# Decode attention with a mixer MLP on one core: K of the filling unit ahead of a batch's last V, queries with wq as weights, a ring of 16 cells

## The chip, the cores and the metric

One core of a Trainium2 chip runs the whole program in one launch. The metric is the device time in microseconds of one execution. Before the change the median of three runs is 2520.77 us (2520.22 to 2522.88).

## What is computed

Two rounds of the same layer pair on two batch rows of 512 numbers: attention over a cached K and V of 32768 places (8 groups of heads, 4 query heads each, 128 numbers a head), then an MLP whose hidden size is 1792 and which works on each number of the row by itself (one token, S = 1). The cache and the weights are the same in both rounds.

```python
x = x + A(layernorm(x))      # attention: q = x @ wq; softmax(q k / sqrt(128)) v; @ wo
x = x + B(layernorm(x))      # u[d, f] = layernorm(x)[d] * w1[f] + b1[f]; gelu(u) @ w2 + b2
x = x + A(layernorm(x))
x = x + B(layernorm(x))
```

K and V are 2 x 2 x 8 x 32768 x 128 floats, 537 MB, and each is read again in the second round.

## The kernel before, in words

A *unit* (layer, batch, group of heads) is the attention of one batch row over one group's cache: 64 cells of K and 64 of V, a cell being 128 partitions x 512 floats (256 KB). There are 32 units. SBUF holds `CELLS` = 105 such cells in one tile, `mem` (line 219). Weights (wq and wo of a group, 8 cells) share it.

The work of the array is a list of 1024 *steps* (class `Order`, line 41), each of four cells: `k_step` (line 315) multiplies four K cells by the unit's query (which stands as weights in `qz`) into scores in PSUM, `v_step` (line 366) multiplies four V cells by the exponentials `S` into `acc`. In general the K steps of a unit stand ahead of the V steps of the unit before, so that the maxima (`max_1`, `max_2`), the transposition of the scores (`turn_scores`, VectorE) and the exponentials (`exponentials`, ScalarE, a half of 32 cells at a time) have other steps beside them. Where K of a unit is followed by its own V, everything hangs on one step: there `p1 == p2` (line 665) and the planner adds 5 us.

Second-round K and V of a batch need the batch's whole first round: the last V of that batch, its output (`take_out`, `out_1`, `out_2`), the layer norm (`mix_1`, `take_rows`, `mix_2`), 14 hidden tiles of 128 x 512 (`hidden_tiles`: gelu on ScalarE, projection on TensorE), `mix_4`, `to_columns`, and the new query (`make_q`). At each of the two places where a batch changes its layer (`changes`), three units take part: x, whose V is the batch's last; the *filling unit* of the other batch, whose steps stand beside the chain; and y, which is the same group and batch as x in the second round and uses again what of x's K and V has stayed in SBUF (`KEPT_K` = 8 cells of K and `KEPT_V` = 64 of V). Before, the order there is: K of x, V of the unit before, first half of the filling unit's K, V of x, second half of the filling unit's K, its V, K of y, V of y.

Small pieces of work are *hooks* put behind chosen steps (function `at`, line 627; from line 659 on for each unit), with an estimate of their time in us. TensorE executes steps and hooks in this order; the other engines get their instructions in the same order.

Loads are planned ahead of time by `plan_loads` (line 112): in the order in which the cells are asked for, each load takes 32, 24, 16, 8 or 4 cells (or the sizes that `cut` has set) at the place where, by the planner's model (`CELL_US`, `LAND_US`, `LEAD_US`, `STEP_US`), DMA would wait least, and is issued by the SP engine right behind the last step that used those cells (lines 722 and 744). Cells that neither hold weights nor stay for y are the ring: near the changes 105 - 72 - 16 = 17 cells, which are loaded four at a time.

`make_q` (line 280) is given one unit or two (both batches of a group): in steps 0 and 1 two matmuls each with the row as weights (128 x n) and wq as the moving operand (512 columns), result n x 512; a copy; in step 2 four transpositions by matmul, and copies into `qz`.

Of the kernel before, what the change touches and what calls it, by code (L numbers as in the profile page):

```python
# [8 lines left out]
F32 = mybir.dt.float32  # L9
AF = mybir.ActivationFunctionType  # L10
# [3 lines left out]
P = 128  # L14
G = 512
# [1 line left out]
STEP = 4  # L17
NG = 4
QT = 4
CELLS = 105  # L20
WCELLS = 8
KEPT_K = 8
KEPT_V = 64
SIZES = (32, 24, 16, 8, 4)
FINAL = (16, 8, 4, 2, 1, 1)
# [7 lines left out]

LOAD_US = 0.12
CELL_US = 0.6024
LAND_US = 1.0
LEAD_US = 2.5
STEP_US = 1.44


class Order:


    def __init__(self, heads):
        far, f, s = list(range(heads - 2)), heads - 2, heads - 1
        self.steps = []
        self.pairs = []
        before = [(0, b, h) for h in far for b in (0, 1)] + [(0, 0, f)]
        x0, fill0, y0 = (0, 0, s), (0, 1, f), (1, 0, s)
        x1, fill1, y1, n = (0, 1, s), (1, 0, f), (1, 1, s), (1, 1, f)  # L50
        after = [(1, b, h) for h in far[:1:-1] for b in (0, 1)] + [(1, b, h) for b in (0, 1) for h in far[1::-1]]
        for i, u in enumerate(before):
            self.k(u)
            if i:
                self.v(before[i - 1])
        self.k(x0), self.v(before[-1]), self.k(fill0, 0), self.v(x0), self.k(fill0, 1), self.v(fill0)
        self.k(y0), self.v(y0), self.k(x1), self.k(fill1, 0), self.v(x1), self.k(fill1, 1), self.v(fill1)
        self.k(y1), self.v(y1), self.k(n)
        prev = n
        for u in after:  # L60
            self.k(u), self.v(prev)
            prev = u
        self.v(prev)
        self.last = prev
        self.changes = ((x0, fill0, y0), (x1, fill1, y1))
        self.units = before + [x0, fill0, y0, x1, fill1, y1, n] + after
        self.first, self.end = {}, {}
        for p, (kind, u, g) in enumerate(self.steps):
# [26 lines left out]

# [99 lines left out]
def gqa_mixer_kernel(ctx: ExitStack, tc: tile.TileContext, x, kt, v, wqo, cols, out):  # L195
# [22 lines left out]
    nc.sync.dma_start(xcols, x)  # L218
    mem = const.tile([P, CELLS * G], F32, name="mem")

    def cells(a, n):
# [52 lines left out]
    def row_tile():  # L274
        return work.tile([P, D], F32, name="row", bufs=1)

    wq_sb, wo_sb = {}, {}
    q_at, q_ps, q_row, turn = {}, {}, {}, [0]

    def make_q(us, step):  # L280

        layer, b, h = us[0]
        n = len(us)
        wq = wq_sb[layer, h] if (layer, h) in wq_sb else wq_sb[0, h]
        if step == 0:
            q_ps[us] = pmisc.tile([P, G], F32, name="misc")
        if step < 2:
            for d in range(step * DT // 2, (step + 1) * DT // 2):
                nc.tensor.matmul(  # L289
                    q_ps[us][:n, :], xn[layer][:, d, b : b + n], wq[:, d, :], start=(d == 0), stop=(d == DT - 1)  # L290
                )
        if step == 1:
            q_row[us] = row_tile()
            nc.vector.tensor_copy(q_row[us][:n, :], q_ps[us][:n, :])  # L294
        if step == 2:
            pt = pmisc.tile([P, G], F32, name="misc")
            for r in range(R):
                nc.tensor.matmul(  # L298
                    pt[:, r * n : (r + 1) * n],
                    q_row[us][:n, r * DH : (r + 1) * DH],  # L300
                    ident[:n, :n],
                    start=True,
                    stop=True,
                )
            for j, u in enumerate(us):
                q_at[u] = 28 + 32 * (turn[0] % SLOTS)
                turn[0] += 1
                nc.vector.tensor_copy(
                    qz[:, q_at[u] : q_at[u] + R], pt[:, : n * R].rearrange("p (r b) -> p b r", b=n)[:, j, :]
                )  # L310

    sc_ps, mx, lsum, oT = {}, {}, {}, {}
    at_cell = {}
# [171 lines left out]
    def gelu_table():  # L485
        t = work.tile([P, 1], F32, name="warm", bufs=1)
        nc.scalar.activation(t, one, AF.Gelu_apprx_tanh)

    hid = {}

# [140 lines left out]
    def queries(us, p0, p1, p2):  # L631
        at(p0, make_q, us, 0, us=1.3)
        at(p1, make_q, us, 1, us=1.3)
        at(p2, make_q, us, 2, us=1.0)

    changed = {y: (x, fill) for x, fill, y in order.changes}
    opening = order.units[0]
# [2 lines left out]
    for u in order.units:  # L640
        layer, b, h = u
        users.setdefault(h if h >= HKV - 2 else (layer, h), []).append(u)
        k0 = first["K", u]
        if u in made and u != opening:
            continue
        mate = (layer, 1, h)
        us = (u, mate) if b == 0 and mate not in made and (layer == 0 or h < HKV - 2) else (u,)
        made.update(us)
        if u == opening:
            opening_q = us  # L650
        elif u not in changed:
# [7 lines left out]
    for u in order.units:  # L659
# [17 lines left out]
        at(v_mid + 2, denominators, u, us=0.2)  # L677
        at(v_end, take_out, u)
        if u == order.last:
            at(v_mid + 4, gelu_table)  # L680
            at(v_mid + 3, mix_1, key, us=0.8)
            at(v_end, out_1, u)
            at(v_end, last_mixer, u)
            continue
        at(v_end + 1, out_1, u, us=1.0)
        at(v_end + 2, out_2, u, us=2.4)
        if u == order.last_of[key]:
            e = v_end
            at(e + 1, mix_1, key, us=0.8)
            at(e + 3, take_rows, key)  # L690
            at(e + 4, mix_2, key, us=0.7)
            g0 = e + 9
            for k in range(FT // 2 + 1):
                at(g0 + k, hidden_tiles, key, k, us=1.0)
            g0 += FT // 2
            at(g0 + 1, take_rows, key)
            at(g0 + 2, mix_4, key, us=0.7)
            if layer == 0:
                at(g0 + 3, to_columns, key, us=0.5)
                (y,) = [y for y, (x, _) in changed.items() if x == u]  # L700
                queries((y,), g0 + 4, g0 + 5, g0 + 6)
                assert g0 + 6 < first["K", y]
# [25 lines left out]
    begin = {}  # L728
    for label, n, a, p in loads:
        begin.setdefault(p, []).append((label, n, a))  # L730
    for label, n, a in begin.get(-1, ())[:1]:
        load(label, n, a)
    nc.sync.dma_start(cols_sb, cols)
    for label, n, a in begin.get(-1, ())[1:]:
        load(label, n, a)
    constants()
    first_input()
    for step in range(3):
# [52 lines left out]
```

## Time and profile before

| | us |
|---|---|
| median of 3 runs | 2520.77 |
| profiled execution | 2520.16 |
| its span, first to last instruction | 2518.4 |
| TensorE busy with matmuls | 1442.3 (57%) |
| TensorE loading weights | 400.0 (16%) |
| VectorE busy | 181.3 (7%) |
| ScalarE busy | 183.7 (7%) |
| from HBM | 1065.38 MB, 423 GB/s over the span |

PE is TensorE's matmuls, PEld its weight loads, DVE VectorE, ACT ScalarE, POOL GpSimd, SP the engine that issues loads. One float32 matmul stands in the trace as two records, so that a step of four cells is 8 records. A row of the timeline has the start, the busy time, engine, line, operation, result and operands, number of records, and in brackets how long the engine was idle before and what ended that. A row of the table of stretches has the stretch and its length, the busy times of PE, PEld, DVE, ACT and POOL (records in brackets), the granted clock of TensorE as a share of full speed, the share of DMA, and GB/s.

### The profile page before, as it was taken

To read this page: it belongs to the slowest core of one execution; us is meant where nothing else is said; L and a number is where in the kernel's file an instruction comes from. 1 tells how busy PE (TensorE), PEld (TensorE's weight loads), DVE (VectorE), ACT (ScalarE), POOL (GpSimd) and SP (SyncE) were. 2 spreads that over 40 slices of the span, in tenths; PEclk is the share of its full clock that TensorE was granted. 3 is DMA by queue.
4 is the path that set the end of the run, shared out by engine and by line. 5 is a ranking of instruction groups with operands and counts; after the bars stand their busy time and mean duration, and the time that the engine had idled before them with its cause. 6 is when DMAs were issued, how large, how long until landed. Compare 5 with 4: busy or idle time off the path is not lost.

```text
span 2518.4 us, 20745 instructions
## 1 busy us (share of the span) xinstructions
PE 1442.3 (57%) x9484; PEld 400.0 (16%) x9484; DVE 181.3 (7%) x473; ACT 183.7 (7%) x572; POOL 4.9 (0%) x16
## 2 busy tenths in 40 slices
PE   4455555655556545557686785455564545565566
PEld 1111111111111111112121221111111111111122
DVE  1000000000000000000100010000000000000011
ACT  0000000000000000002011101000000000000021
POOL 0000000000000000000000000000000000000000
PEclk7777777777767777778887787777777777777777
DMA  9999999999999999999999999999999999999996
GB/s 416 432 436 434 434 431 432 431 431 431 431 433 433 433 435 433 418 435 396 403 427 398 397 425 430 438 434 431 431 433 433 434 430 438 434 426 433 426 430 258
DMA packets 33792, 1066.71 MB, mean 424 GB/s; under 512 B 4005, under 2 KB 4009, under 8 KB 4394
## 3 DMA queue, kind: packets, MB, share of 16 engines
q1 hardware_dynamic: 33700, 1065.40, 98.8%
q8 instruction: 74, 1.21, 0.2%
q14 instruction: 12, 0.10, 0.0%
q10 hardware_dynamic: 6, 0.00, 0.0%
HBM read 1065.38 MB, written 0.00 MB: 423 GB/s over the span
## 4 chain that ended last, share of the span: by engine, by line
DMA 67%; PE 31%; ACT 1%; DVE 1%; issue 0%; SPq 0%; POOLq 0%; ACTq 0%; DVEq 0%
DMA mem<-in_kt_dram 36%; DMA mem<-in_v_dram 30%; PE acc L375 12%; PE scores L322 12%; PE misc L420 2%; PE rows L437 2%; PE misc L289 1%; ACT S L357 0%; PE rows L493 0%; PE misc L346 0%; PE misc L340 0%; PE bcast L457 0%; PE acc L592 0%; PE misc L539 0%; PE bcast L519 0%
## 5 line engine op out<-in xcount | busy, mean ns | idle before, releaser
L375 PE MATMUL acc<-mem,S 128*16 128x512 f32 x4092 | 626.7, 711 | 523.0 <-DMA mem<-in_v_dram 513.3
L322 PE MATMUL scores<-mem,qz 128*32 128x512 f32 x4096 | 613.4, 734 | 524.9 <-DMA mem<-in_kt_dram 524.8
L357 ACT ACTIVATE S<-S,neg 128x128 f32<-128x128 f32 x256 | 129.6, 509 | 2247.1 <-DVE S L352 1180.9
L322 PEld LDWEIGHTS scores<-mem,qz 128*32 128x32 f32 x4096 | 136.8, 128 | 926.0 <-DMA mem<-in_kt_dram 469.2
L375 PEld LDWEIGHTS acc<-mem,S 128*16 128x16 f32 x4092 | 129.9, 106 | 848.3 <-issue 793.1
L332 DVE TENSOR_REDUCE mx<-scores 128x1 f32<-128x512 f32 x64 | 44.3, 692 | 827.9 <-PE scores L322 827.9
L289 PE MATMUL misc<-mem,xn 128*2 128x512 f32 (+1 forms) x144 | 86.9, 737 | 4.3 <-DMA mem<-in_wqo_dram 4.3
L420 PEld LDWEIGHTS misc<-selg,row 128*128 128x128 f32 x256 | 50.8, 295 | 46.8 <-issue 41.6
L352 DVE STREAM_TRANSPOSE S<-scores 128x512 f32<-128x512 f32 x64 | 45.5, 711 | 140.7 <-PE acc L375 140.7
L420 PE MATMUL misc<-selg,row 128*128 128x4 f32 x256 | 53.6, 333 | 0.6 <-DVE row L405 0.6
L437 PE MATMUL rows<-mem,oT 128*1 128x512 f32 x248 | 52.1, 931 | 0.0
L357 ACT ACTIVATION_READ_ACCUMULATOR S<-S,neg 128x1 f32 x256 | 47.7, 187 | 0.0
L493 PE MATMUL rows<-hid,cols_sb 128*1 128x512 f32 x84 | 33.8, 616 | 1.0 <-ACT hid L508 1.0
L342 DVE TENSOR_REDUCE m<-misc 1x4 f32<-1x128 f32 x32 | 8.9, 278 | 342.4 <-PE misc L340 342.4
L415 DVE COPY row<-acc 128x512 f32<-128x512 f32 x31 | 21.5, 692 | 149.7 <-PE acc L375 149.7
L508 ACT ACTIVATE hid<-bcast,bias,scale 128x512 f32<-128x512 f32 x42 | 30.4, 774 | 17.0 <-PE rows L493 8.6
L289 PEld LDWEIGHTS misc<-mem,xn 128*2 128x2 f32 (+1 forms) x144 | 14.5, 101 | 74.2 <-issue 72.9
L428 DVE TENSOR_TENSOR oT<-misc,rl 128x4 f32<-128x4 f32 x32 | 5.2, 162 | 283.6 <-PE misc L420 283.6
L294 DVE COPY row<-misc 2x512 f32<-2x512 f32 (+1 forms) x18 | 12.2, 679 | 183.5 <-PE misc L289 123.0
L340 PE MATMUL misc<-ident,mxa 128*1 128x128 f32 x64 | 17.8, 375 | 5.1 <-DVE mxa L338 5.1
L401 DVE RECIPROCAL rl<-misc 128x4 f32<-128x4 f32 x32 | 5.9, 183 | 197.4 <-PE misc L399 197.4
L298 PEld LDWEIGHTS misc<-ident,row 2*128 2x128 f32 (+1 forms) x144 | 17.3, 186 | 16.2 <-issue 12.7
(92 smaller groups left out, 204.0 us busy)
## 6 DMA issues: line engine op xcount, KB each, us to landing
mem<-in_kt_dram SPq DMA_DIRECT2D x27, 2048.0 KB, 13.0
mem<-in_v_dram SPq DMA_DIRECT2D x37, 1024.0 KB, 8.2
mem<-in_kt_dram SPq DMA_DIRECT2D x32, 1024.0 KB, 9.4
mem<-in_wqo_dram SPq DMA_DIRECT2D x14, 2048.0 KB, 33.1
mem<-in_v_dram SPq DMA_DIRECT2D x3, 6144.0 KB, 26.7
mem<-in_v_dram SPq DMA_DIRECT2D x8, 2048.0 KB, 10.4
mem<-in_v_dram SPq DMA_DIRECT2D x4, 4096.0 KB, 38.0
mem<-in_kt_dram SPq DMA_DIRECT2D x4, 4096.0 KB, 17.2
```

Source lines behind the costliest of these rows:

```text
L289: nc.tensor.matmul(q_ps[us][:n, :], xn[layer][:, d, b : b + n], wq[:, d, :], start=(d == 0), stop=(d == DT - 1))
L322: nc.tensor.matmul(sc_ps[u, half][32 * row : 32 * row + 32, :], qz[:, at : at + 32], cells(at_cell["K", u, g], 1), start=(i == 0), stop=(i ...
L332: nc.vector.tensor_reduce(mx[u][:, half : half + 1], sc_ps[u, half], axis=AX.X, op=ALU.max)
L340: nc.tensor.matmul(pm[:1, :P], mxa, ident, start=True, stop=True)
L352: nc.vector.transpose(S[half], sc_ps[u, half])
L357: nc.scalar.activation(s[:, :, h], s[:, :, h], AF.Exp, bias=neg[u][:, h : h + 1], scale=SCALE, accum_out=lsum[u][:, half, h : h + 1],)
L375: nc.tensor.matmul(acc[32 * row : 32 * row + R * QT, :], S[half][:, col : col + R * QT], vc, start=(g < NG), stop=(g >= quads - NG),)
L415: nc.vector.tensor_copy(asb[u], acc)
L420: nc.tensor.matmul(po[:, :R], asb[u][:, t * DH : (t + 1) * DH], selg[:, t * R : (t + 1) * R], start=(t == 0), stop=(t == QT - 1),)
L437: nc.tensor.matmul(rows[b][32 * r : 32 * r + 1, :], oT[u][:, r : r + 1], wo_of(u)[:, r, :], start=(u == order.first_of[layer, b]), stop=(u ...
L493: nc.tensor.matmul(rows[key[1]][32 * g : 32 * g + 1, :], w2c[:, f : f + 1], hid.pop((key, f)), start=(f < NG), stop=(f >= FT - NG),)
L508: nc.scalar.activation(hid[key, f], px[key], AF.Gelu_apprx_tanh, bias=shift[key][:, f : f + 1], scale=slope[key][:, f : f + 1],)
```

## The change

- The order at a change of layer is now: K of x, V of the unit before, all of the filling unit's K, V of x, V of the filling unit, K of y, V of y. Behind V of x the chain thus has the 16 V steps of the filling unit, where it had 8 K steps and 16 V steps.
- The chain's hooks move closer together: `mix_1` two steps ahead of V's end, `out_1` right at V's end, `out_2`, `take_rows` and `mix_2` behind the next two steps, one pair of hidden tiles a step from the fourth step on, the query in steps 14 and 15 (counted from V's end). ScalarE is told to load its gelu table, and afterwards its exp table, ahead of use.
- `make_q` takes 128 x 128 pieces of wq as weights and the row's columns (128 x n) as moving operand: 16 matmuls in two steps, whose result needs no transposition; a copy into `qz` is left.
- `KEPT_K` becomes 10 (74 cells stay), `CELLS` 106, and the ring at the changes 106 - 74 - 16 = 16. The 106th cell's space comes from the hidden tiles, of which one of two now uses the row buffer.
- The planner's `LAND_US` goes from 1.0 to 1.1 and `LEAD_US` from 2.5 to 1.8.
- x and the columns of w1, b1 and w2 are loaded by ScalarE's queue instead of SP's.

```diff
-CELLS = 105
+CELLS = 106
-KEPT_K = 8
+KEPT_K = 10
-LAND_US = 1.0
-LEAD_US = 2.5
+LAND_US = 1.1
+LEAD_US = 1.8
...
-        self.k(x0), self.v(before[-1]), self.k(fill0, 0), self.v(x0), self.k(fill0, 1), self.v(fill0)
-        self.k(y0), self.v(y0), self.k(x1), self.k(fill1, 0), self.v(x1), self.k(fill1, 1), self.v(fill1)
+        self.k(x0), self.v(before[-1]), self.k(fill0), self.v(x0), self.v(fill0)
+        self.k(y0), self.v(y0), self.k(x1), self.k(fill1), self.v(x1), self.v(fill1)
...
-        for x, fill, _ in self.changes:
+        for x, fill, y in self.changes:
+            self.cut("K", y, KEPT_K, (-KEPT_K % STEP,))
             self.cut("V", x, HALF, TAPER)
-            self.cut("K", fill, HALF, (STEP,) * 8)
             self.cut("V", fill, 0, (STEP,) * 16)
...
-    hidden = ctx.enter_context(tc.tile_pool(name="hidden", bufs=2))
+    hidden = ctx.enter_context(tc.tile_pool(name="hidden", bufs=1))
...
-    nc.sync.dma_start(xcols, x)
+    nc.scalar.dma_start(xcols, x)
...
-        if step < 2:
-            for d in range(step * DT // 2, (step + 1) * DT // 2):
+        for r in range(step * R // 2, (step + 1) * R // 2):
+            for d in range(DT):
                 nc.tensor.matmul(
-                    q_ps[us][:n, :], xn[layer][:, d, b : b + n], wq[:, d, :], start=(d == 0), stop=(d == DT - 1)
+                    q_ps[us][:, r * n : (r + 1) * n],
+                    wq[:, d, r * DH : (r + 1) * DH],
+                    xn[layer][:, d, b : b + n],
+                    start=(d == 0),
+                    stop=(d == DT - 1),
                 )
         if step == 1:
-            q_row[us] = row_tile()
-            nc.vector.tensor_copy(q_row[us][:n, :], q_ps[us][:n, :])
-        if step == 2:
-            pt = pmisc.tile([P, G], F32, name="misc")
-            for r in range(R):
-                nc.tensor.matmul(
-                    pt[:, r * n : (r + 1) * n],
-                    q_row[us][:n, r * DH : (r + 1) * DH],
-                    ident[:n, :n],
...
-                hid[key, f] = hidden.tile([P, D], F32, name="hid")
+                hid[key, f] = hidden.tile([P, D], F32, name="hid") if f % 2 else row_tile()
...
-            queries(us, k0 - 10, k0 - 8, k0 - 6)
+            queries(us, k0 - 8, k0 - 6)
...
-        at(v_end + 1, out_1, u, us=1.0)
-        at(v_end + 2, out_2, u, us=2.4)
-        if u == order.last_of[key]:
-            e = v_end
-            at(e + 1, mix_1, key, us=0.8)
-            at(e + 3, take_rows, key)
-            at(e + 4, mix_2, key, us=0.7)
-            g0 = e + 9
-            for k in range(FT // 2 + 1):
-                at(g0 + k, hidden_tiles, key, k, us=1.0)
-            g0 += FT // 2
-            at(g0 + 1, take_rows, key)
-            at(g0 + 2, mix_4, key, us=0.7)
-            if layer == 0:
-                at(g0 + 3, to_columns, key, us=0.5)
-                (y,) = [y for y, (x, _) in changed.items() if x == u]
-                queries((y,), g0 + 4, g0 + 5, g0 + 6)
+        if u != order.last_of[key]:
+            at(v_end + 1, out_1, u, us=1.2)
+            at(v_end + 2, out_2, u, us=2.0)
+            continue
+        e = v_end
+        at(e - 2, mix_1, key, us=1.2)
+        at(e, out_1, u, us=1.9)
+        at(e + 1, out_2, u, us=2.0)
+        at(e + 1, take_rows, key)
+        at(e + 2, mix_2, key, us=1.2)
+        at(e + 2, table, AF.Gelu_apprx_tanh)
+        for k in range(FT // 2 + 1):
+            at(e + 4 + k, hidden_tiles, key, k, us=1.2)
+        e += 4 + FT // 2
+        at(e, take_rows, key)
+        at(e, table, AF.Exp)
+        at(e + 1, mix_4, key, us=1.2)
+        if layer == 0:
+            at(e + 2, to_columns, key, us=1.0)
+            (y,) = [y for y, (x, _) in changed.items() if x == u]
+            queries((y,), e + 3, e + 4)
...
-    nc.sync.dma_start(cols_sb, cols)
+    nc.scalar.dma_start(cols_sb, cols)
```

More of the change, by code (lines that the diff above doesn't have):

```diff
@@ L277, in gqa_mixer_kernel @@
     wq_sb, wo_sb = {}, {}
-    q_at, q_ps, q_row, turn = {}, {}, {}, [0]
+    q_at, q_ps, turn = {}, {}, [0]
     def make_q(us, step):
@@ L286, in make_q @@
             q_ps[us] = pmisc.tile([P, G], F32, name="misc")
-        if step < 2:
-            for d in range(step * DT // 2, (step + 1) * DT // 2):
+        for r in range(step * R // 2, (step + 1) * R // 2):
+            for d in range(DT):
                 nc.tensor.matmul(
-                    q_ps[us][:n, :], xn[layer][:, d, b : b + n], wq[:, d, :], start=(d == 0), stop=(d == DT - 1)
+                    q_ps[us][:, r * n : (r + 1) * n],
[3 more added lines that the diff above has]
+                    stop=(d == DT - 1),
                 )
         if step == 1:
-            q_row[us] = row_tile()
-            nc.vector.tensor_copy(q_row[us][:n, :], q_ps[us][:n, :])
-        if step == 2:
-            pt = pmisc.tile([P, G], F32, name="misc")
-            for r in range(R):
-                nc.tensor.matmul(
-                    pt[:, r * n : (r + 1) * n],
-                    q_row[us][:n, r * DH : (r + 1) * DH],
-                    ident[:n, :n],
-                    start=True,
-                    stop=True,
-                )
+            q = q_ps[us][:, : n * R].rearrange("p (r b) -> p b r", b=n)
             for j, u in enumerate(us):
@@ L307, in make_q @@
                 turn[0] += 1
-                nc.vector.tensor_copy(
-                    qz[:, q_at[u] : q_at[u] + R], pt[:, : n * R].rearrange("p (r b) -> p b r", b=n)[:, j, :]
-                )
+                nc.vector.tensor_copy(qz[:, q_at[u] : q_at[u] + R], q[:, j, :])
     sc_ps, mx, lsum, oT = {}, {}, {}, {}
@@ L483, in mix_2, with table @@
         nc.vector.scalar_tensor_tensor(shift[key], slope[key], off, b1c, op0=ALU.mult, op1=ALU.add)
-    def gelu_table():
+    def table(func):
         t = work.tile([P, 1], F32, name="warm", bufs=1)
-        nc.scalar.activation(t, one, AF.Gelu_apprx_tanh)
+        nc.scalar.activation(t, one, func)
     hid = {}
@@ L629, in at, with queries @@
         busy[p] = busy.get(p, 0.0) + us
[L631 to L634, printed above, removed]
+    def queries(us, p0, p1):
+        at(p0, make_q, us, 0, us=2.2)
+        at(p1, make_q, us, 1, us=2.2)
     changed = {y: (x, fill) for x, fill, y in order.changes}
@@ L679, in gqa_mixer_kernel @@
         if u == order.last:
-            at(v_mid + 4, gelu_table)
+            at(v_mid + 4, table, AF.Gelu_apprx_tanh)
             at(v_mid + 3, mix_1, key, us=0.8)
@@ L684, in gqa_mixer_kernel @@
             continue
-        at(v_end + 1, out_1, u, us=1.0)
-        at(v_end + 2, out_2, u, us=2.4)
-        if u == order.last_of[key]:
-            e = v_end
-            at(e + 1, mix_1, key, us=0.8)
-            at(e + 3, take_rows, key)
-            at(e + 4, mix_2, key, us=0.7)
-            g0 = e + 9
-            for k in range(FT // 2 + 1):
-                at(g0 + k, hidden_tiles, key, k, us=1.0)
-            g0 += FT // 2
-            at(g0 + 1, take_rows, key)
-            at(g0 + 2, mix_4, key, us=0.7)
-            if layer == 0:
-                at(g0 + 3, to_columns, key, us=0.5)
-                (y,) = [y for y, (x, _) in changed.items() if x == u]
-                queries((y,), g0 + 4, g0 + 5, g0 + 6)
-                assert g0 + 6 < first["K", y]
+        if u != order.last_of[key]:
[19 more added lines that the diff above has]
+            queries((y,), e + 3, e + 4)
+            assert e + 4 < first["K", y]
     loads = plan_loads(order, weights, busy)
@@ L730, in gqa_mixer_kernel @@
         begin.setdefault(p, []).append((label, n, a))
-    for label, n, a in begin.get(-1, ())[:1]:
-        load(label, n, a)
-    nc.sync.dma_start(cols_sb, cols)
-    for label, n, a in begin.get(-1, ())[1:]:
+    nc.scalar.dma_start(cols_sb, cols)
+    for label, n, a in begin.get(-1, ()):
         load(label, n, a)
@@ L737, in gqa_mixer_kernel @@
     first_input()
-    for step in range(3):
+    for step in range(2):
         make_q(opening_q, step)
```

## Prediction, made before the changed kernel ran

> **What bounds the kernel now.** I read the page first (chain of work, GB/s in 40 slices), then a table of stretches, then the timeline of PE around the two changes of layer.
>
> ```profile
> DMA 67%; PE 31%; ACT 1%; DVE 1%; issue 0%; SPq 0%; POOLq 0%; ACTq 0%; DVEq 0%
> DMA  9999999999999999999999999999999999999996
> GB/s 416 432 436 434 434 431 432 431 431 431 431 433 433 433 435 433 418 435 396 403 427 398 397 425 430 438 434 431 431 433 433 434 430 438 434 426 433 426 430 258
> ```
>
> The chain that ended last is loads. Away from three places they run at one rate: slice 1 (start), slices 19 to 24, and the last slice (the tail, which this change leaves as it is). So a microsecond counts only if DMA moves fewer bytes or is held up less. The stretches, with rate in the last column (the numbers before it are the share of DMA, the granted clock and the busy times):
>
> ```profile
> 60.00:1140.00 1080.00, 585.85 (x3846) 162.13 (x3850) 64.86 (x167) 59.16 (x224) 0.00 (x0) 0.73 1.00 432
> 1160.00:1178.00 18.00, 12.71 (x70) 2.48 (x62) 4.17 (x12) 0.90 (x3) 0.54 (x1) 0.69 0.97 378
> 1178.00:1192.00 14.00, 12.23 (x67) 2.61 (x68) 0.00 (x0) 11.77 (x25) 0.00 (x0) 0.79 0.96 365
> 1192.00:1207.00 15.00, 10.69 (x59) 2.52 (x56) 2.58 (x7) 4.18 (x5) 0.54 (x1) 0.91 1.01 426
> 1207.00:1224.00 17.00, 17.00 (x110) 5.97 (x110) 2.11 (x6) 0.00 (x0) 0.00 (x0) 0.88 0.97 371
> 1224.00:1246.00 22.00, 10.76 (x68) 1.69 (x64) 1.31 (x2) 0.00 (x0) 0.00 (x0) 0.77 1.00 400
> 1360.00:1378.00 18.00, 12.99 (x70) 2.25 (x62) 3.57 (x12) 0.00 (x0) 0.54 (x1) 0.69 0.98 383
> 1378.00:1396.00 18.00, 15.17 (x80) 3.33 (x80) 0.60 (x1) 14.83 (x31) 0.00 (x0) 0.80 0.90 339
> 1409.00:1422.00 13.00, 13.00 (x78) 4.48 (x82) 2.11 (x6) 0.00 (x0) 0.00 (x0) 0.86 0.95 367
> 1422.00:1446.00 24.00, 14.64 (x92) 2.66 (x88) 1.31 (x2) 0.00 (x0) 0.00 (x0) 0.66 1.00 408
> ```
>
> 432 GB/s is the steady rate: a cell (128x512 floats, 262144 bytes) takes 0.607 us, a load of four 2.43 us. Length times (1 - rate/432) is what a stretch loses. **A**, the head of the chain between the layers: 2.25 and 2.04. **B**, softmax of the filling unit and the first MLP tiles: 2.17 and 3.88. **D**, back to columns and the query: 2.40 and 1.96. **E**, K of the next layer: 1.63 and 1.33. Together 17.7 us.
>
> Why it is lost there: only a ring of 16 to 17 cells is left, loaded four at a time, and the quickest load of all took 4.6 us to land:
>
> ```profile
> DMA to landing us min/median/max: 4.6/26.8/42.8
> ```
>
> Four slots give 4 x 2.43 = 9.7 us, less 4.6 leaves 5.1 us from a load's landing until PE has let its cells go, or the queue runs dry. Less its own transfer, a load needs 2.2 us from issue.
>
> ```profile
> 1154.97 1.06 PE L322 MATMUL scores<-mem,qz 128*32 128x512 f32 x8 [1.44 <-DMA mem<-in_kt_dram]
> 1157.19 2.05 PE L457 MATMUL bcast<-ident,xcols 128*128 128x128 f32 x8
> 1160.88 1.93 PE L437 MATMUL rows<-mem,oT 128*1 128x512 f32 x8
> ...
> 1172.33 1.94 PE L322 MATMUL scores<-mem,qz 128*32 128x512 f32 x8 [0.88 <-DMA mem<-in_kt_dram]
> ...
> 1179.26 3.62 PE L375 MATMUL acc<-mem,S 128*16 128x512 f32 x16 [2.46 <-ACT S L357]
> ```
>
> B is the clearest: the last K step starts at 1172.33, softmax follows it with nothing of another unit between, the next step starts at 1179.26 and, at 1.81 us a step, lets its cells go at about 1181.1. That is 8.8 us, 3.7 beyond the 5.1.
>
> **The change part by part.** It is summed against the profiled execution's 2520.16 us (span 2518.4 and 1.8 around it); the median, 2520.77, stands 0.6 above.
>
> *Cells kept.* KEPT_K goes from 8 to 10 at two changes: 4 cells less are read, 4 x 0.607 = **-2.4**.
>
> *Start.*
>
> ```profile
> 0.74 0.41 SPq L218 DMA_DIRECT2D xcols<-in_x_dram  x1
> 1.20 0.42 SPq L715 DMA_DIRECT2D mem<-in_wqo_dram  x1
> ```
>
> x and cols go to ACT's queue, and the first weights become SP's first issue: 1.20 to 0.74, **-0.5**. ACT issues both ahead of its first table load; their cover is the first K, which PE gets only at 28.5 us in the timeline's row below.
>
> ```profile
> 28.56 9.54 PE L322 MATMUL scores<-mem,qz 128*32 128x512 f32 x64 [12.08 <-DMA mem<-in_kt_dram]
> ```
>
> *K of the filling unit ahead.* The second half of its K now runs before the last V of the batch, so its maxima and its first exponentials lie inside V steps that wait for DMA anyway. The 5.1 us gap between PE's rows at 1174.3 and 1179.26 goes, at both changes. What is late next is the head of the chain, now in front of V instead of K: take_out's copy (0.69), out_1, a step, out_2, a step, mix_2, a step; mix_1 (2.05) has gone ahead into V steps. With
>
> ```profile
> 1153.61 0.69 DVE L415 COPY row<-acc 128x512 f32<-128x512 f32 x1 [8.43 <-PE acc L375]
> 1155.97 1.36 PE L420 MATMUL misc<-selg,row 128*128 128x4 f32 x8
> 1164.81 1.12 PE L471 MATMUL bcast<-row,selg 128*128 128x512 f32 x2
> ```
>
> and 1.05 a step, reloads are issued 3.3, 6.3 and 8.5 us after V's end (0.2 for semaphores). In before the first ring load was used 1.44 us after V's end, so three more end at about 1.44 + 7.3 = 8.7; less 2.2, the reloads are due at 6.5, 8.9 and 11.4. All are in time by 2.4 us or more. Bounds: nothing left, or A as it is (4.3). I take 0.7 for each change, as queues this short lose a little: A and B fall from 10.3 to 1.4, **-8.9**. The MLP tiles take 1.05 for a step and 1.09 for two projections, under 2.43:
>
> ```profile
> 1196.01 1.09 PE L493 MATMUL rows<-hid,cols_sb 128*1 128x512 f32 x4
> 1200.10 1.05 PE L375 MATMUL acc<-mem,S 128*16 128x512 f32 x8 [1.34 <-DMA mem<-in_v_dram]
> 1204.17 0.39 PE L399 MATMUL misc<-both,one 128*128 128x4 f32 x2 [1.96 <-DVE both L398]
> 1204.48 1.91 PE L375 MATMUL acc<-mem,S 128*16 128x512 f32 x8
> 1206.32 1.87 PE L539 MATMUL misc<-ident,row 128*128 128x1 f32 x8
> ...
> 1209.80 2.14 PE L289 MATMUL misc<-mem,xn 128*1 128x512 f32 x3
> ...
> 1215.73 1.05 PE L298 MATMUL misc<-ident,row 1*128 1x1 f32 x8
> ...
> 1219.44 1.05 PE L420 MATMUL misc<-selg,row 128*128 128x4 f32 x8
> ```
>
> The even tiles go into the row buffer, free by then (mix_2 has read it), so two buffers remain. Table loads stay eight in the program; the two inside the chains are only asked for earlier.
>
> *Queries with wq as weights.* No row has this shape (128x128 weights, one or two columns moving). 16 matmuls are 32 records; nearest are L420 (1.05/8 = 0.131 us a record) and, at the low clock, L539 (1.87/8 = 0.234): 4.2 or 7.5 us. Removed are 8 records of L289 (2.14 for three, at most 6 us for all), a copy and 8 of L298 (1.05), 6 to 7 us. In the steady stretches this lies in PE's slack; price zero. In D it counts. [...]
>
> *D, compressed.* Denominators now come before mix_4, so PE's wait of 1.96 us behind DVE goes. From the landing of mix_4's step, PE does four steps (4.2), L519 (1.12, as L471), columns (1.05 to 1.87) and the first half query (2.1 to 3.7): the next load of the ring goes out at 8.5 to 10.9 us. Queued until then are three loads of the ring, 7.3 us, and 10 cells more, 6.1; less 2.2, it is due at 11.2. The second half query and one step end at 11.6 to 15.7, due at 13.6. So nothing is lost at the high clock, 2.1 a change if only the new matmuls run at the low one, and more if the V steps do too; the other end is D as it is, 4.4 for both. I take 1.0 a change, nearer to the high clock, because projections now keep PE busy until just before: D from 4.4 to 2.0, **-2.4**.
>
> *E.* 26 cells instead of 25 and smaller loads; bounds 0 and 3.0; I take 2.4, **-0.6**.
>
> *New tight gates.* The planner's LEAD 1.8 lets a few loads wait for one step more: second K half after the first step of its first half, a V load before the change, the last 16 cells of V after steps of their own unit instead of the unit before. The first has eight cells of weights behind it (4.85 us), less a cold step (1.94) and 2.2: just in time. Bounds 0 and 3 x 2.2; I take **+0.4**.
>
> Sum: 2520.2 - 2.4 - 0.5 - 8.9 - 2.4 - 0.6 + 0.4 = **2505.8**, written as 2506.
>
> **Rivals.**
>
> *Low clock in D.* PE's eight records took 1.05 at 1200.10 and 1.91 at 1204.48. If columns, query and part of the steps run at the latter, D keeps 3.0 a change (+4.0) and A and B, where out_1 is then 0.5 longer, 1.4 (+1.4): **2511**. For it: before shows just this at 1204 to 1210. Against: that was after a 1.96 us wait that goes. [...]
>
> *Nearly all goes.* A, B, D and E keep 1.5 in all: 2505.8 - 4.3 = **2501.5**. For it: every reload above is in time.
>
> *The loss only moves.* The chain has V alone behind it, 64 cells or 38.8 us, where it had 96 or 58.3. If V's steps are held up as K's were, only cells and start count: **2517.3**. Against: B's gap has a cause that is gone.
>
> *Slower.* 13 of the 18 queries (L298's 144 records are 8 each) lie in the V half ahead of a K load of 32 cells.
>
> ```profile
> 133.03 2.76 PE L289 MATMUL misc<-mem,xn 128*2 128x512 f32 x3
> ...
> 135.59 0.79 PE L289 MATMUL misc<-mem,xn 128*2 128x512 f32 x1
> ...
> 138.52 1.05 PE L298 MATMUL misc<-ident,row 2*128 2x2 f32 x8
> ...
> 150.73 1.94 PE L322 MATMUL scores<-mem,qz 128*32 128x512 f32 x8 [6.75 <-DMA mem<-in_kt_dram]
> ```
>
> ```profile
> L298 PE MATMUL misc<-ident,row 2*128 2x2 f32 (+1 forms) x144 | 18.9, 248 | 0.8 <-DVE row L294 0.8
> L420 PE MATMUL misc<-selg,row 128*128 128x4 f32 x256 | 53.6, 333 | 0.6 <-DVE row L405 0.6
> ```
>
> There PE waits 6.75 us for the next K half; the load that it has just let go needs 2.2, so 4.5 us are spare. If a record cost its mean of 0.333 one after another, 32 take 10.7 instead of the 4.6 of the three rows in that half: 6.1 more, 1.6 beyond the spare, 13 times 21 us, and some 5 at each change: 2505.8 + 21 + 10 = **2537**. It decides from 0.285 us a record (9.1 / 32). Against: 0.131 to 0.234 start to start.
>
> **How the numbers follow.** Forecast 0.56 (2503 to 2509), low clock 0.16, nearly all 0.14, loss moves 0.07, slower 0.07. 2500 to 2515 holds the first three, 0.86 less their edges. 0.2% is 5 us, about what a measurement of this kernel tells from no change: faster (under 2515.7) 0.86, same 0.07, slower 0.07.
>
> **What would show it.** Right: no wait of PE on ACT S in V near 1180 and 1380; the rate over the two changes (1160 to 1246, 1360 to 1446) above 420; MLP tiles at one step in 2.43 us; L289 with 32 records in 4 to 7.5 us; PE waits for K half loads still above 2.2 in the steady stretches. Wrong: slices under 425 before 1100 or after 1500 (queries or gates), or PE steps of V with projections further apart than 2.43 us.

## The result, and the profile after

The kernel after took 2543.01 us (median of 4, 2528.71 to 2553.05) beside 2521.82 (2520.22 to 2524.5, 4 runs) for the kernel before on the same chip: a ratio of 1.0077 with a 95% interval of 1.0053 to 1.0102. It is slower by 0.8%, where 2506 had been forecast. It also varies: before, runs lie within 0.2%, after, within 1%. The profiled execution, 2528.71 us with a span of 2526.9, is the quickest of the four; its granted clock is 0.751, that of the other three 0.735 to 0.738.

First the page of the kernel after, its shares of the chain that ended last and its slices.

```profile
DMA 69%; PE 29%; issue 0%; DVE 0%; ACT 0%; SPq 0%; POOLq 0%; POOL 0%; DVEq 0%; ACTq 0%
GB/s 416 430 430 433 430 431 432 420 438 426 418 437 394 432 432 431 423 434 419 397 421 425 402 427 440 430 429 433 434 423 435 395 430 434 432 414 430 431 430 274
```

Loads still end last. But holes stand where before had none: slices 8, 11, 13, 32 and 36 (394 to 420 GB/s, where before had 426 or more), all far from the changes of layer. The table of stretches shows the exchange (columns as in the prediction: stretch, length, busy times, granted clock, share of DMA, GB/s). Before:

```profile
60.00:1160.00 1100.00, 600.52 (x3952) 167.40 (x3956) 66.67 (x172) 59.16 (x224) 0.00 (x0) 0.73 1.00 431
1160.00:1246.00 86.00, 63.39 (x366) 15.27 (x358) 10.17 (x27) 16.84 (x32) 1.09 (x2) 0.80 0.98 388
1246.00:1360.00 114.00, 79.08 (x556) 21.68 (x560) 9.54 (x24) 8.31 (x32) 0.00 (x0) 0.83 1.01 427
1360.00:1446.00 86.00, 64.42 (x362) 15.51 (x358) 10.16 (x27) 16.84 (x32) 1.08 (x2) 0.76 0.97 385
1446.00:1500.00 54.00, 47.61 (x322) 13.23 (x318) 6.08 (x16) 4.13 (x16) 0.00 (x0) 0.84 1.00 425
1500.00:2480.00 980.00, 531.11 (x3496) 148.53 (x3488) 62.70 (x160) 69.03 (x226) 0.54 (x1) 0.75 1.00 432
```

After:

```profile
60.00:1160.00 1100.00, 593.31 (x3970) 189.00 (x3970) 60.78 (x162) 59.26 (x224) 0.00 (x0) 0.73 0.99 427
1160.00:1246.00 86.00, 68.61 (x456) 22.10 (x456) 10.44 (x29) 17.40 (x34) 1.09 (x2) 0.87 0.97 400
1246.00:1360.00 114.00, 72.42 (x523) 21.54 (x523) 8.20 (x21) 8.29 (x32) 0.00 (x0) 0.79 1.00 424
1360.00:1446.00 86.00, 67.81 (x442) 20.95 (x434) 10.16 (x28) 17.39 (x34) 1.08 (x2) 0.86 1.00 412
1446.00:1500.00 54.00, 46.68 (x366) 17.79 (x366) 4.81 (x14) 4.16 (x16) 0.00 (x0) 0.88 1.00 415
1500.00:2480.00 980.00, 536.14 (x3540) 165.85 (x3540) 59.28 (x155) 67.22 (x223) 0.54 (x1) 0.73 0.99 428
```

By length times (1 - rate/432), the two changes (rows 2 and 4) lose 10.4 us instead of 18.1, and the stretches behind them (rows 3 and 5) 4.2 instead of 2.2. The long steady stretches (rows 1 and 6) lose 21.8 instead of 2.5: 19 us that the prediction had put at nothing. In all 13.6 more, less 2.4 for cells and 0.5 at the start, is 10.7; measured is 8.6 (the rates are rounded, and half a GB/s over 1000 us is 1.2 us).

**Where the steady loss arises.** PE's timeline of the kernel after, in a V half that holds a query (start, busy, line, operands, records, wait):

```profile
778.30 1.91 PE L366 MATMUL acc<-mem,S 128*16 128x512 f32 x8 [9.79 <-DMA mem<-in_v_dram]
780.14 3.58 PE L289 MATMUL misc<-xn,mem 128*128 128x2 f32 x16
783.65 1.91 PE L366 MATMUL acc<-mem,S 128*16 128x512 f32 x8
...
787.84 3.58 PE L289 MATMUL misc<-xn,mem 128*128 128x2 f32 x16
791.35 7.22 PE L366 MATMUL acc<-mem,S 128*16 128x512 f32 x40
798.39 1.03 PE L313 MATMUL scores<-mem,qz 128*32 128x512 f32 x8
...
821.72 3.64 PE L313 MATMUL scores<-mem,qz 128*32 128x512 f32 x16 [14.27 <-DMA mem<-in_kt_dram]
```

The same half in the kernel before:

```profile
773.26 1.91 PE L375 MATMUL acc<-mem,S 128*16 128x512 f32 x8 [8.35 <-DMA mem<-in_v_dram]
774.92 2.76 PE L289 MATMUL misc<-mem,xn 128*2 128x512 f32 x3
...
779.33 1.05 PE L375 MATMUL acc<-mem,S 128*16 128x512 f32 x8
780.31 1.05 PE L298 MATMUL misc<-ident,row 2*128 2x2 f32 x8
781.29 4.49 PE L375 MATMUL acc<-mem,S 128*16 128x512 f32 x40
792.61 1.93 PE L322 MATMUL scores<-mem,qz 128*32 128x512 f32 x8 [6.83 <-DMA mem<-in_kt_dram]
```

Read the steps, and not the query alone. A step of eight records takes 1.91 at half clock and 1.05 at full clock. Before, the clock has risen by 779.33 and the half's eight steps end at 785.8, 12.5 us after they began; then PE waits 6.83 us for K. After, steps stay at 1.91 up to 791.35 and the half ends at 798.4, 20.1 us after it began; K's first step waits for nothing, and the K half behind it waits 14.27. Counted from start to start, the query takes 7.0 us of the half for 3.2 before, and the eight steps 12.6 for 9.0. What happened in between stands in SP's rows. After, then before:

```profile
768.57 30.40 SPq L716 DMA_DIRECT2D mem<-in_kt_dram  x2
```

```profile
764.99 21.18 SPq L722 DMA_DIRECT2D mem<-in_kt_dram  x2
```

Each row holds two K loads; the second is issued when the V half has let its cells go, at 768.57 + 30.40 = 798.97 after and at 786.17 before. 20 us is more than the queue has to move: one K load of 32 cells, 19.4 us. DMA runs dry (kernel after):

```profile
785.00:795.00 10.00, 10.00 (x50) 4.95 (x50) 0.41 (x3) 0.00 (x0) 0.00 (x0) 0.50 0.83 356
795.00:800.00 5.00, 5.00 (x38) 1.40 (x30) 1.31 (x2) 0.00 (x0) 0.00 (x0) 0.81 0.55 184
800.00:805.00 5.00, 5.00 (x48) 1.76 (x52) 0.16 (x1) 2.16 (x8) 0.00 (x0) 1.00 0.58 249
```

Here 6.7 us are lost (1.8, 2.9 and 2.1), about 5 net of the rates of 452 to 485 in the stretches around them. The granted clock of 0.50 in the first row says the same as the steps. The clock rises only during the five steps in a row at 791.35, which take 7.22 (5 x 1.91 = 9.6 at half clock, 4.49 at full clock before).

**At the changes** the chain's head went as forecast. PE in the kernel after, at the end of the batch's last V:

```profile
1178.36 1.91 PE L366 MATMUL acc<-mem,S 128*16 128x512 f32 x16 [0.43 <-DMA mem<-in_v_dram]
...
1185.20 1.15 PE L411 MATMUL misc<-selg,row 128*128 128x4 f32 x8 [0.82 <-DVE row L406]
...
1198.25 1.05 PE L366 MATMUL acc<-mem,S 128*16 128x512 f32 x8 [0.60 <-DMA mem<-in_v_dram]
1200.73 1.05 PE L366 MATMUL acc<-mem,S 128*16 128x512 f32 x8 [0.53 <-DMA mem<-in_v_dram]
```

No wait on ACT is left; steps of the MLP start 2.48 us apart, each on its landing. But the query of the next layer, same kernel:

```profile
1218.11 1.05 PE L366 MATMUL acc<-mem,S 128*16 128x512 f32 x8 [0.44 <-DMA mem<-in_v_dram]
1219.09 2.63 PE L289 MATMUL misc<-xn,mem 128*128 128x1 f32 x16
1221.65 1.91 PE L366 MATMUL acc<-mem,S 128*16 128x512 f32 x8
1223.49 3.57 PE L289 MATMUL misc<-xn,mem 128*128 128x1 f32 x16
```

```profile
1178.00:1222.00 44.00, 35.60 (x230) 11.12 (x234) 6.73 (x19) 15.24 (x26) 1.09 (x2) 0.94 1.01 421
1222.00:1240.00 18.00, 15.90 (x104) 6.55 (x96) 1.01 (x3) 0.00 (x0) 0.00 (x0) 0.77 0.87 330
```

The clock was high at 1218.11 (1.05 for eight records) and fell within the first half of the query (1.91 at 1221.65), with PE busy all the time. Up to 1222 the rate is 421 GB/s; behind the query it is 330, 4.3 us lost.

### The profile page after: what moved, and what is told of

The parts are those of the page before. It is cut to its first block, busy times and chain, and to the rows that moved or that the text cites. A ratio compares the mean times of both kernels' runs of the same rounds, so it can differ in the third digit from the quotient of the medians.

```text
span 2526.9 us, 21280 instructions
## 1 busy us (share of the span) xinstructions
PE 1443.1 (57%) x9772; PEld 462.0 (18%) x9772; DVE 169.1 (7%) x455; ACT 185.4 (7%) x578; POOL 4.9 (0%) x16
## 4 chain that ended last, share of the span: by engine, by line
DMA 69%; PE 29%; issue 0%; DVE 0%; ACT 0%; SPq 0%; POOLq 0%; POOL 0%; DVEq 0%; ACTq 0%
DMA mem<-in_v_dram 36%; DMA mem<-in_kt_dram 34%; PE acc L366 13%; PE scores L313 11%; PE misc L289 4%; PE misc L390 0%; PE misc L411 0%; PE rows L428 0%; PE rows L484 0%; PE acc L583 0%; ACT S L348 0%; ACT mem L593 0%; PE misc L337 0%; PE misc L331 0%; PE bcast L462 0%
## 5 line engine op out<-in xcount | busy, mean ns | idle before, releaser
L366 PE MATMUL acc<-mem,S 128*16 128x512 f32 x4092 | 616.1, 734 | 552.3 <-DMA mem<-in_v_dram 547.4
L313 PE MATMUL scores<-mem,qz 128*32 128x512 f32 x4096 | 589.4, 716 | 505.2 <-DMA mem<-in_kt_dram 505.2
L366 PEld LDWEIGHTS acc<-mem,S 128*16 128x16 f32 x4092 | 124.3, 107 | 866.7 <-issue 793.6
L289 PEld LDWEIGHTS misc<-xn,mem 128*128 128x128 f32 x576 | 101.7, 274 | 50.9 <-issue 49.2
L289 PE MATMUL misc<-xn,mem 128*128 128x2 f32 (+1 forms) x576 | 104.6, 312 | 1.8 <-issue 1.8
L484 PE MATMUL rows<-row,cols_sb 128*1 128x512 f32 x42 | 24.0, 655 | 0.6 <-ACT row L499 0.6
L484 PE MATMUL rows<-hid,cols_sb 128*1 128x512 f32 x42 | 23.6, 646 | 0.0
L390 PEld LDWEIGHTS misc<-both,one 128*128 128x128 f32 x64 | 13.9, 270 | 48.3 <-issue 47.4
L499 ACT ACTIVATE row<-bcast,bias,scale 128x512 f32<-128x512 f32 x21 | 16.3, 778 | 38.9 <-PE rows L484 18.1
```

The costliest lines, as they stand in the source:

```text
L289: nc.tensor.matmul(q_ps[us][:, r * n : (r + 1) * n], wq[:, d, r * DH : (r + 1) * DH], xn[layer][:, d, b : b + n], start=(d == 0), stop=(d ...
L313: nc.tensor.matmul(sc_ps[u, half][32 * row : 32 * row + 32, :], qz[:, at : at + 32], cells(at_cell["K", u, g], 1), start=(i == 0), stop=(i ...
L366: nc.tensor.matmul(acc[32 * row : 32 * row + R * QT, :], S[half][:, col : col + R * QT], vc, start=(g < NG), stop=(g >= quads - NG),)
L484: nc.tensor.matmul(rows[key[1]][32 * g : 32 * g + 1, :], w2c[:, f : f + 1], hid.pop((key, f)), start=(f < NG), stop=(f >= FT - NG),)
L499: nc.scalar.activation(hid[key, f], px[key], AF.Gelu_apprx_tanh, bias=shift[key][:, f : f + 1], scale=slope[key][:, f : f + 1],)
```

## The experiments

The theory (**N**, for narrow): matmuls with one or two moving columns do not keep the clock up or bring it up, though they fill PE's timeline; steps beside them stay at half clock, the V half lasts too long, and the next K load is late. The first rival (**G**, for gates): the shorter LEAD makes loads wait for a step more. Others: the new place of the query's halves, its 32 weight loads as mere work for PE (**W**), its access pattern. Runs of one chip share their runs of the kernel before: 2523.29 us beside e1 to e4, 2523.39 beside e5 to e7, 2522.3 beside e8 to e11. Between chips only ratios are compared.

**e1, the old query in the kernel after.** wq moves again, 512 columns, in three steps.

```diff
-            queries(us, k0 - 8, k0 - 6)
+            queries(us, k0 - 10, k0 - 8, k0 - 6)
```

> The changed kernel with the query made as before (row as weights, 512 columns of wq moving, three steps); everything else as changed. Theory N (the narrow query matmuls, 1 or 2 columns moving, do not keep the array's clock up, so that the V half around them runs at half clock and lets its cells go late): no V half with a query takes over 14 us, the stretch 60 to 1160 runs at 431 or more GB/s, 2505 to 2511 us, and single runs lie within 5 us of each other. Rival W (the 32 weight loads are simply more work for PE): the same time. Rival G (the planner's shorter lead lets loads go out too late): still 2528 to 2553 with a wide spread.

Measured 2513.22 (2511.75 to 2514.97), ratio 0.9958 (0.9946 to 0.9970). All but the query's form brings 10 us; the form costs 30.

**e2, the new query alone in the kernel before.** `make_q` as in the change, everything else as before.

```diff
-            queries(us, k0 - 10, k0 - 8, k0 - 6)
+            queries(us, k0 - 8, k0 - 6)
```

> The kernel before with the query's new form alone (16 matmuls in two steps, 8 and 6 steps ahead of K). Theory N and rival W: slower than before by 8 to 30 us, 2528 to 2550, with a spread of 10 us or more between runs, and loads of K halves behind queries late. Rival G: 2515 to 2524, no spread, since lead and order are those of before.

Measured 2556.89 (2547.68 to 2560.78), ratio 1.0124 (1.0105 to 1.0143), at a granted clock of 0.729. The form alone costs 31 us, with the old lead, order and ring. In the profiled execution twelve steady queries took 3.58 us in each of their halves, the low clock; in the kernel after a first half at 3.58 is sometimes followed by a second at 1.95.

**e3, wide columns.** The kernel after, each moving column repeated to 128 by a stride of zero; of the 128 results one copy is used. Weights, their 32 loads, places and gates are those of after.

```diff
+    def again(a, n):
+        return bass.AP(a.tensor, a.offset, [a.ap[0], [0, P // n], [a.ap[-1][0], n]])
...
-                    xn[layer][:, d, b : b + n],
+                    again(xn[layer][:, d, b : b + n], n),
```

> The changed kernel with the same 16 query matmuls and weight loads, but the moving columns repeated to 128 (a stride of zero), so that the array has 128 columns to work on behind each weight load instead of 1 or 2; the query is read from the first copy. PE's work per record is no less. Theory N: the clock rises in V halves with a query as it did before, a half takes 10 to 14 us, 2505 to 2513 us, spread under 6. Rival W and rival G: no better than the changed kernel, 2528 to 2553.

Measured 2512.22 (2510.91 to 2515.27), ratio 0.9957 (0.9945 to 0.9970). With 64 or 128 times as many columns to multiply, it is 1.2% faster than the kernel after. PE's timeline of e3 in the half shown above:

```profile
774.46 1.91 PE L369 MATMUL acc<-mem,S 128*16 128x512 f32 x8 [9.20 <-DMA mem<-in_v_dram]
776.30 3.79 PE L292 MATMUL misc<-xn,mem 128*128 128x128 f32 x16
780.02 1.31 PE L369 MATMUL acc<-mem,S 128*16 128x512 f32 x8
...
782.56 2.05 PE L292 MATMUL misc<-xn,mem 128*128 128x128 f32 x16
784.54 4.48 PE L369 MATMUL acc<-mem,S 128*16 128x512 f32 x40
794.03 1.78 PE L316 MATMUL scores<-mem,qz 128*32 128x512 f32 x8 [5.01 <-DMA mem<-in_kt_dram]
```

The first half of the query is no quicker (3.79, for 3.58 narrow), but 6 us after the half began the clock is up: the step behind it takes 1.31, and the second half 2.05. The half ends at 789.0, and PE waits 5.01 us for K again. In all twelve steady halves of e3 that begin at the low clock the second half of the query takes 2.05. The steady stretches of e3 run at the rate of before, for 427 and 428 in the kernel after:

```profile
60.00:1160.00 1100.00, 590.48 (x4000) 185.77 (x4004) 61.06 (x163) 59.12 (x224) 0.00 (x0) 0.73 1.00 431
1500.00:2480.00 980.00, 530.09 (x3560) 160.93 (x3556) 58.15 (x154) 69.34 (x228) 0.54 (x1) 0.74 1.00 431
```

They lose 4.8 us for 21.8. The two changes are no better in e3's profiled execution, at 409 and 402 GB/s: 10.6 us lost for 10.4. (That execution is the slowest of its five, the one of the kernel after the quickest of its four.)

**e4, the old lead in the kernel after,** narrow columns.

```diff
-LAND_US = 1.1
-LEAD_US = 1.8
+LAND_US = 1.0
+LEAD_US = 2.5
```

> The changed kernel with the planner's LAND 1.0 and LEAD 2.5 of before; queries stay narrow. Theory N and rival W: 2526 to 2553 and a wide spread, as with the changed kernel, perhaps 2 us better. Rival G: 2505 to 2511, no spread.

Measured 2539.25 (2527.86 to 2544.62), ratio 1.0057 (1.0038 to 1.0075). The intervals of this and of after overlap: G explains no more than a few us, and falls as the cause.

**e5, wide columns and the old lead:** the edits of e3 and e4 together.

> Repeated columns (128 wide) and the planner's LAND 1.0 and LEAD 2.5 of before together. Theory N says the queries cost nothing more; then the lead is seen without them: the tight loads near 1040 to 1080 and between the layers (1240 to 1280, 1417 to 1447) keep 1 to 3 us, so 2508 to 2512 against 2510.9 to 2515.3 with the short lead. Rival (the lead plays no part, what is left is the ring): within 1 us of the short lead.

Measured 2509.06 (2507.12 to 2511.20), ratio 0.9946 (0.9934 to 0.9958): the best version, 14 us under before. The two changes in e5:

```profile
1160.00:1246.00 86.00, 64.77 (x448) 18.81 (x440) 9.99 (x27) 17.46 (x34) 1.09 (x2) 0.90 1.00 416
...
1360.00:1446.00 86.00, 63.31 (x427) 18.32 (x431) 11.14 (x30) 17.72 (x36) 1.08 (x2) 0.88 1.01 416
```

They lose 3.2 us each, 6.4 in all, for 18.1 before.

**e6 and e11, how wide.** The kernel after with columns repeated to 8, 32 and 64. Of the three expectations below, the first (8 columns) was written as an addition to the second (32).

```diff
-        return bass.AP(a.tensor, a.offset, [a.ap[0], [0, P // n], [a.ap[-1][0], n]])
+        return bass.AP(a.tensor, a.offset, [a.ap[0], [0, WIDE // n], [a.ap[-1][0], n]])
```

> [...] If few columns are enough: 2510 to 2516.

> The changed kernel with the query's moving columns repeated to 32 instead of 128. [...] If any more than a few columns count as work, it is as with 128: 2510 to 2516.

> The kernel after with its moving columns repeated to 64. 1, 2, 8 and 32 columns gave 2543 to 2545, 128 gave 2512. Clock theory gives no threshold: 2540 or above if 64 columns count as little as 32 do, 2512 to 2515 if they count as 128 do; in between if halves differ from one another. Rival, that the cost lies in some other property of the narrow form (one access pattern against the repeated one): 32 repeated columns have already spoken against it; 64 near 2512 would make the width alone decide.

| columns | us, median | ratio to before, 95% |
|---|---|---|
| 1 or 2 (after) | 2543.01 | 1.0077 (1.0053 to 1.0102) |
| 8 | 2544.45 | 1.0075 (1.0047 to 1.0102) |
| 32 | 2542.74 | 1.0078 (1.0064 to 1.0092) |
| 64 | 2536.19 | 1.0065 (1.0039 to 1.0091) |
| 128 (e3) | 2512.22 | 0.9957 (0.9945 to 0.9970) |

Repeating columns is not what helps: 8, 32 and 64 have the same kind of access pattern as 128. In this kernel the width decides, and somewhere between 64 (1.0065) and 128 (0.9957). The profiled executions agree: of twelve steady queries the second half ran at the low clock in 10 with 8 columns, in 7 with 32, in 7 with 64 (16 records in 3.68 us) and in none with 128. At the two changes, where the clock is high when the query begins, it stayed up both times with 64 columns (2.00 in each half), and once each with 8 (1.95) and 32 (1.97).

**e7, narrow and spread.** The steady queries of the kernel after in eight pieces of two matmuls, one behind each of eight steps, so that no stretch of narrow matmuls is longer than 1 us.

```diff
-            queries(us, k0 - 8, k0 - 6)
+            for j in range(8):
+                at(k0 - 10 + j, make_q, us, j, 8, us=0.6)
```

> The changed kernel with narrow queries, but away from the changes of layer made in eight pieces of two matmuls behind eight steps in a row (10 to 3 steps ahead of K) instead of two pieces of eight. Theory N with a share over a window: 4 records (0.85 us at half clock) between steps of 1.7 us leave two thirds of the time busy, so the clock rises in most halves and the time is 2512 to 2522, with a spread under 10. Rival (a narrow matmul anywhere in the window holds the clock down): 2530 or more. Rival W (it is work): 2528 or more.

Measured 2563.61 (2561.77 to 2567.11), ratio 1.0162 (1.0148 to 1.0176): the worst of all. Here N, as it was put then, was wrong: it took a short piece among steps to be harmless. The rival that a narrow matmul anywhere nearby holds the clock down had the right side (2530 or more); so had W, which e3 rules out. PE in e7:

```profile
793.61 1.91 PE L366 MATMUL acc<-mem,S 128*16 128x512 f32 x8 [8.95 <-DMA mem<-in_v_dram]
795.45 1.01 PE L289 MATMUL misc<-xn,mem 128*128 128x2 f32 x4
...
809.78 1.01 PE L289 MATMUL misc<-xn,mem 128*128 128x2 f32 x4
810.73 3.61 PE L366 MATMUL acc<-mem,S 128*16 128x512 f32 x16
```

Steps of 1.91 and pieces of 1.01 alternate for 17 us, and the clock does not rise at all until they end. Two thirds wide steps and one third narrow matmuls were not enough to raise it in this half.

**e8, eight cells kept.** e5 with the ring still at 16 cells (and without the `cut` of y's first K load, which eight cells don't need).

```diff
-CELLS = 106
-KEPT_K = 10
+CELLS = 104
+KEPT_K = 8
```

> The version with wide query columns and the old lead, with KEPT_K back at 8 and CELLS at 104, so that the ring has its 16 cells still. Cells theory: 4 cells more are read, 4 x 0.607 = 2.4 us, so some 2511.5 beside a kernel before of 2523 (ratio 0.9956 where that version had 0.9946). Rival, that 10 kept cells bring something at the change beyond their bytes (K's first half then starts from the chip): 2513 or more. Rival, that they bring nothing: 2509.

Measured 2511.45 (2509.92 to 2512.01), ratio 0.9956 (0.9944 to 0.9968) for e5's 0.9946: 2.5 us by the medians of the ratio. The intervals overlap, so the size agrees with 4 cells of 0.607 but is not settled by it.

**e9, the kernel before with a wide new query:** the edits of e2 and of e3.

> The kernel before with the new query alone, its moving columns repeated to 128. Clock theory: the form of the query costs nothing when the array's clock stays up, so within 3 us of the kernel before (2520 to 2526 beside 2523), where the narrow query alone stood 31 us above it. Rival, that something else in the new form costs (its 32 weight loads a query, the place of its two halves): half or more of the 31 us stay, 2538 or above.

Measured 2522.31 (2519.88 to 2525.53, 12 runs), ratio 1.0002 (0.9994 to 1.0010). All of e2's 31 us go with the width; weight loads, places and copies of the new form cost nothing that shows. The long steady stretches run at 431 GB/s, where 60 to 1160 and 1500 to 2480 in e2 had 424 and 426.

**e10, e5 with narrow queries at the two changes only.**

```diff
+        w = n if us[0] in [y for _, _, y in order.changes] else P
```

> The version with wide columns and the old lead, but with narrow columns (one) for the two queries at the changes of layer alone. Clock theory: those queries run in V steps of the next unit at the low clock and only the two stretches behind them lose: in the kernel after 1222 to 1240 ran at 330 GB/s and 1417 to 1447 at 393, 4.3 and 2.7 us against 432, where the wide version lost 0 and 1.1; so 3 to 6 us above 2509, 2512 to 2515 beside 2523. Rival, that narrow queries cost only in the steady halves: 2509.

Measured 2514.59 (2511.12 to 2515.64), ratio 0.9966 (0.9954 to 0.9979): 5 us above e5 by the ratios, whose intervals barely overlap. The profile puts it where it was expected: the steady stretches stay at 431, and the two changes run at 401 and 400 GB/s, 12.5 us lost for e5's 6.4. PE in e10 at the first change:

```profile
1208.20 1.05 PE L370 MATMUL acc<-mem,S 128*16 128x512 f32 x8 [0.63 <-DMA mem<-in_v_dram]
1209.18 2.98 PE L293 MATMUL misc<-xn,mem 128*128 128x1 f32 x16
1212.09 1.91 PE L370 MATMUL acc<-mem,S 128*16 128x512 f32 x8
```

Again the clock falls within the first half of the query (eight records in 1.05 us, then in 1.91).

## Why the prediction was wrong

**The step that failed** is the one on queries with wq as weights: "In the steady stretches this lies in PE's slack; price zero." PE's time for the query was sized rightly: 16 records took 1.95 us at full and 3.58 at half clock, 0.122 and 0.224 a record, for the forecast's 0.131 and 0.234. What was missed is what the query does to the steps beside it. The half clock holds, the V half takes up to 7.6 us longer (20.1 for 12.5: 3.8 in the query, 3.6 in its eight steps, the rest in L390), and the slack was 4.5: some 3 us are lost by this sum, about 5 in the half shown. By the same sum the query alone, even at half clock, would have fitted into the slack.

The new form costs 1.20% with narrow columns and nothing with 128 (e1, e3, e9): 30 us, of which e10 puts 5 at the changes; the other 25, over the prediction's 13 V halves, are 1.9 each. That split is one for the old lead; with the short one the profiled executions of after and e3 lose alike at the changes, so there it stays open.

The 25 are not lost evenly. Twelve steady queries (the thirteenth, at 1471, begins at the high one) of the kernel after begin at the low clock in its profiled execution: in seven the clock rose ahead of the query's second half, in five it stayed low, and in e2 it stayed low in all twelve. Three of the five (near 780, 1985 and 2232) stand at the holes of slices 13, 32 and 36. The other two, near 945 and 2150, cost nothing (431 and 432 GB/s over the 80 us around them): there eight cells of weights, 4.9 us, were queued behind the K load, which agrees with the account by slack. The smaller holes of slices 8 and 11 follow halves of 15.5 and 15.9 us in which the clock rose; other halves as long lost nothing, and why is open. That the clock rises more often in one execution than in the next was not traced; the granted clock, 0.751 in the quickest of the four and 0.735 to 0.738 in the others, fits it.

The prediction's own signs told the place: slices under 425 before 1100 and after 1500 were to mean queries or gates. The rate over the two changes, 400 and 412, did not reach the 420 that was to show it right.

**The rival "Slower"** named the place (the V half ahead of a K load) and the slack of 4.5 us, and had the right sign, but not the mechanism: it needed records of 0.285 us, and they never cost that. Its 2537 is near 2543 by accident.

**A and B** (10.3 to 1.4): the mechanism was right. PE waits for ACT no longer, and 1160 to 1222 and 1360 to 1400 in the kernel after lose 3.3 us (406 GB/s up to 1178, 421 up to 1222, 420 from 1360), so 7.0 of the 8.9 came, with the first query matmuls already among what is left.

**D** (4.4 to 2.0): wrong in the kernel after for the same reason. The rival "Low clock in D" had the place and nearly the price: it added 4.0 there (5.4 with A and B), and e10 measured 5. It looked for the cause in a wait ahead of the query; here the clock fell during the query itself. In the kernel after it rose within the five steps in a row at 791.35, which took 7.22 us, for 9.6 at half clock. PE's rows without a gap did not keep it up: from 1218.11 PE had no idle time, and a step went from 1.05 us to 1.91 at 1221.65.

**Cells kept** (-2.4): e8 gives 2.5. Its intervals would allow nothing as well as twice as much. **Start** (-0.5): the first weights are issued at 0.74 us for 1.20, as forecast. **E** (-0.6) can't be read by itself. **New tight gates** (+0.4): e5, with the old lead, is 2.8 us below e3 by the ratios, within the bounds of 0 to 6.6, with intervals that overlap. So the term was probably too small.

**The sum** without the failed step was nearly sound. e3, which differs from the change in width alone, stands 0.43% (0.30 to 0.55) under before, 7.6 to 13.9 us, where 14.4 were forecast: 3 to 4 short at its median, most of it perhaps the gates. e5, with the old lead too, stands 0.54% (0.42 to 0.66) under, 10.6 to 16.7 us. A, B, D and E were to fall from 17.7 to 5.8; e5 loses 6.4 at the two changes for 18.1, e3 10.6.

That the number of moving columns decides is shown, by e3, e6, e9 and e11. Why it does is not shown. Why the clock rises in some narrow halves and not in others stays open too.

## What to carry to other kernels

A matmul's price was its time and also what it did to the clock of the matmuls around it: steps beside the narrow query took 1.91 us, for 1.05 at full clock. Before swapping operands so that a few columns move past 128 x 128 weights, ask what the steps beside it cost at half clock, and whether the next load waits for their end; slack of 4.5 us, measured at the high clock, was not slack here at the low one, where the V half took up to 7.6 us longer. If the form is wanted, repeat the columns to 128 by a stride of zero: here that cost 0.1 to 0.2 us a half and took 30 us away.

## What the runs showed that was not expected

- In the steady V halves the clock rose no more often with 8 to 64 moving columns than with two: of twelve second halves of the query 10 ran at the low clock with 8 columns, 7 with 32, 7 with 64, and 5 with two (kernel after); with 128, none.
- One record of the query took nearly the same time with 2 or 128 columns moving: 16 took 1.95 and 2.05 us at full clock, 3.58 and 3.79 at half.
- The clock fell under a busy timeline: steps of 1.05 us at 1218.11 became 1.91 at 1221.65, with nothing but narrow matmuls between. It did not always: the queries at 1294, 1471 and 1491 in the kernel after, behind 56 to 72 records of steps in a row, kept 1.95 in both halves.
- Spreading narrow matmuls among wide ones was worse than keeping them together: 2563.61 (e7) for 2543.01, on different chips, with ratios 1.0162 and 1.0077.
